# Two gated linear attentions on one core: the last stage rewritten as one list of steps in a joint order of all engines

## The chip, the cores and the metric

The kernel runs on one core of one Trainium2 chip. A core has a matrix engine (PE, whose weight loads the profile counts apart as PEld), a vector engine (DVE), a scalar engine (ACT), GpSimd (POOL) and a sync engine (SP). Here SP only issues transfers; ACT issues some besides its own work. Each engine works through its own instructions in the order in which they were written, and waits on semaphores for what the others must have done. The metric is the time of one execution in microseconds of device time; a time is the median over several executions.

## The reference, cut to what matters

Two branches A and B with weights of their own see the same input `x` of 2048 tokens by 448. Both are linear attentions with 16 heads of 28, and a gate mixes them:

```
qkv = x @ wqkv                        # per head: q, k, v of 28
pq, pk = q @ w_phi, k @ w_phi         # per head
phi = concat(softmax(p), softmax(-p)) # 56 features for q, and for k
kv, z = phi_k^T v, sum of phi_k
o = (phi_q kv) / (phi_q z + 1e-6)
a = o @ wo                            # branch A; b is branch B in the same way
out = g * a + (1 - g) * b,   g = sigmoid(sum(x * gate_w))
```

All is float32. Where the kernel multiplies by weights, it splits an operand into a high and a low part and adds three products.

## The kernel before, in words

The 2048 tokens are 16 tiles of 128, and the work goes by pairs of tiles, units 0 to 7 (`NU` = 8). The program has three stages.

The first makes branch A's keys and values. The second makes branch A's queries and its attention result unit by unit, and stores it to device memory (`od`), while branch B's keys and values are accumulated in PSUM. Both hold three PSUM pairs (tiles of two banks, `two`) that are used in turn, and two banks for the state `kv`.

The last stage makes branch B's queries and attention, joins A's and B's results (the gate is already in the weights of each), and multiplies by `wo`. Its steps for a unit `u` and its two tiles `t` = 2u and 2u+1:

- `proj`: 22 matmuls make a unit's projected queries in a PSUM pair. `q_front` takes the maximum of every head (DVE) and the differences to it (DVE, two instructions, into `uq`), and stores them by four transfers, two from SP and two from ACT. `q_load` reads them back in another layout (`tq`, SP).
- `q_exp0`, `q_min`, `q_exp1`, `q_turn`: ACT takes exponents, DVE the minimum, POOL the negated differences, ACT their exponents, and DVE turns the result by 32x32 blocks into `wtb`.
- `num`: the product of the features with the turned state `kvt` (PE, 32 matmuls over four banks). `b_turn` turns it back (DVE) into `ctr` or into a part of `wva`, which takes the place of a second `ctr`. `n_rec`, `n_den` and `weights` make the divisor and the gate's weights (DVE and POOL in turns).
- `b_mix`: for each tile POOL multiplies by the weights (`n_mul`, 896 columns) and adds the two halves into `osb` (`n_add`), beside which A's result has been loaded (`o_load`, SP).
- `o_turn`: DVE turns a tile's joined result, four of seven 128-column parts into a PSUM bank (`turned`, tile `pair`) and three into SBUF or into the first bank of `num`; ACT copies each as the high part. `low_first` (DVE) and `low_rest` (POOL for even tiles, DVE for odd ones) make the low part.
- `out_mm`: 21 matmuls, 7 high by high weights, 7 high by low weights, 7 low by high weights (`woh`, `wol`). `out_copy`: ACT copies the product to `obs`, SP stores it.

The order of the engines' work is the order in which Python calls these functions. At the start of the last stage the pools of the first two are closed and a new pool `stage3` takes their place: two pairs, whose first bank holds a product and whose second a turned tile, and four banks `num`. Then a loop takes the units one by one, and within it stands the whole of one unit's chain:

```
        if u <= NU:
            low_first(2 * u - 2)
        if u < NU:
            b_num(u)
        out_mm(2 * u - 3)
        if u < NU:
            b_turn(u)
```

Of the kernel before, what the change touches and what calls it, by code (L numbers as in the profile page):

```python
# [8 lines left out]
F32 = mybir.dt.float32  # L9
# [5 lines left out]
P = 128  # L15
# [9 lines left out]
WARM = 16  # L25
MID = 4


@with_exitstack
def hedgehog_mix(ctx: ExitStack, tc: tile.TileContext, xd, wv, wkt, wqt, wphi, wo, cmask, cpmask, out):  # L30
# [6 lines left out]
    one_stack, two_stack = ExitStack(), ExitStack()  # L37
    one = one_stack.enter_context(tc.tile_pool(name="one", bufs=1, space=bass.MemoryType.PSUM))
    two = two_stack.enter_context(tc.tile_pool(name="two", bufs=3, space=bass.MemoryType.PSUM))
# [78 lines left out]
    def two_tile():  # L118
        return two.tile([P, 2, 512], F32, name="two")
# [49 lines left out]
    def k_sums(k):  # L169
# [5 lines left out]
        nc.vector.reciprocal(rs, sm)  # L175
        phis[k] = es.pop(k)
        for s in range(2):
            e3 = e[:, s].rearrange("p (h f) -> p h f", f=DH)
            nc.gpsimd.tensor_tensor(e3, e3, rs[:, s, :, None].to_broadcast([P, HA, DH]), OP.mult)  # L179

# [7 lines left out]
    kvb = [one.tile([P, 512], F32, name=f"kv{b}") for b in range(2)]  # L188
    for b in range(2):
        nc.vector.memset(kvb[b], 0.0)  # L190
    kvp = [t[:, :H * DH // 2].rearrange("p (g s f) -> p g s f", g=4, f=DH) for t in kvb]
# [16 lines left out]
    def state_turn(b):  # L208
        nc.vector.transpose(kvt[b].rearrange("p s g m -> p (s g m)"), kvs[b].rearrange("p s g f -> p (s g f)"))

        nc.gpsimd.memset(kvt[b][:, :, :, DH + 1], 1.0)
        nc.gpsimd.tensor_scalar(kvt[b][:, 0, :, DH], kvt[b][:, 0, :, DH], 1e-6, None, op0=OP.add)

# [4 lines left out]
    def q_front(k, ps):  # L218
# [8 lines left out]
        for c in range(4):  # L227
            eng = nc.sync if c < 2 else nc.scalar
            eng.dma_start(qd[k][:, :, c].rearrange("r t x -> t r x"), u[32 * c:32 * c + 32].rearrange("p r g w f -> p r (g w f)"))

# [11 lines left out]
    def q_min(k):  # L242
        mn = work.tile([P, 4, 8], F32, name="qmn")
        nc.vector.tensor_reduce(mn, tq[k % 2].rearrange("p c g w f -> p c (g w) f"), AX.X, OP.min)  # L244
        nc.gpsimd.tensor_tensor(eq[:, 1, :, :, :DH], mn.rearrange("p c a -> p a c")[:, :, :, None].to_broadcast([P, 8, 4, DH]),  # L245
                                tview(k), OP.subtract)

# [26 lines left out]
    def n_rec(k):  # L274
        rs, dd, den = sms[k] = sums()
        cv = cview(k)
        nc.vector.reciprocal(rs, cv[:, :, :, :, DH + 1])  # L277
        nc.gpsimd.tensor_tensor(dd, cv[:, :, :, :, DH], rs, OP.mult)  # L278
        nc.gpsimd.tensor_tensor(den, dd[:, :, 0], dd[:, :, 1], OP.add)

# [220 lines left out]
    k, n, m = 2 * NU - 1, NU - 1, NU + 1  # L501
# [4 lines left out]
    def o_load(u):  # L506
        nc.sync.dma_start(osb[:, u % 2, :, 0:4, :], od[u].rearrange("p (a r f) -> p a r f", r=4, f=DH))

    pq = proj(2, wq[1], two_tile())
    k_sums(k)  # L510
    a_turn(n)
    n_rec(n)
    q_front(NU + 2, pq)
    q_load(NU + 2)
    q_exp0(m)
    q_min(m)
    q_exp1(m)
    n_den(n)
    pq = proj(3, wq[1], two_tile())
    kv_acc(k)  # L520
    state_copy(1)
    q_front(NU + 3, pq)
    q_load(NU + 3)
    state_turn(1)
    weights(n, nc.gpsimd)
    n_mul(n)
    a_add(n)
    q_turn(m)
    for u in range(2):
        o_load(u)  # L530
# [8 lines left out]
    hls = {}  # L539

    def turned(t, ps, lo, hi):

# [3 lines left out]
        nc.scalar.activation(hls[t][0][:, lo:hi], ps, AF.Copy)  # L546

    def low(t, ps, lo, hi, eng):
        eng.tensor_tensor(hls[t][1][:, lo:hi], ps, hls[t][0].bitcast(F32)[:, lo:hi], OP.subtract)  # L549


    def turn_of(t):
        return pairs[t % 2][:, 1].rearrange("p (k t) -> p k t", t=P)

    def rest_of(t):
        return nps[:, 0, :(7 - MID) * P].rearrange("p (k t) -> p k t", t=P) if t % 2 and t > 1 else oTs[t % 2]

    def o_turn(t):
        if t % 3 == 2:
            hls[t] = [ph.tile([P, 7, P], F32R, name=f"vs{i}", bufs=1) for i in range(2)]  # L560
        else:
            e = ph.tile([P, 2, 7, P], F32R, name="e")
            hls[t] = [e[:, i] for i in range(2)]
        turned(t, turn_of(t), 0, MID)
        turned(t, rest_of(t), MID, 7)

    def low_first(t):
        low(t, turn_of(t), 0, MID, nc.vector)

    def low_rest(t, eng):  # L570
        low(t, rest_of(t), MID, 7, eng)

    def out_mm(t):
        hi, lo = hls.pop(t)
        terms = [(x[:, c], w[:, c]) for x, w in ((hi, woh), (hi, wol), (lo, woh)) for c in range(7)]
        for n, (a, w) in enumerate(terms):
# [144 lines left out]
```

## Time and profile before

| | |
|---|---|
| time, median of 3 runs | 373.44 us (372.65 to 373.65) |
| profiled execution | 371.96 us, of which the span is 369.9 us |
| PE busy in the span | 349.8 us (95%) |
| DVE, POOL, ACT busy | 274.8 us (74%), 258.7 us (70%), 120.5 us (33%) |
| TensorE clock granted | 1.00 in the whole span |
| last stage, on PE | 245.12 us (its first projection) to 366.5 us (its last product) |

The profile is of one execution. A row of the timeline says when a group of like instructions starts, how long it lasts, the engine, the line in the kernel, what is written and read, and in brackets how long the engine stood idle before it and what released it. The chain of waits goes back from the last instruction, at each step to what released it. A line number belongs to the function printed above that holds it.

### The profile page before, as it was taken

The page shows a single profiled execution, that of the slowest core. Times are in us where ns is not written, and L with a number is a line of the kernel's source. Part 1 is how long each engine was busy: PE and PEld are TensorE (multiplying, and loading weights), DVE is VectorE, ACT ScalarE, POOL GpSimd, SP SyncE. Part 2 cuts the span into 40 slices and gives each one's busy share as a digit, 9 for nine tenths or more (in the row PEclk, how much of TensorE's full clock was granted, in tenths as well). Part 3 has the DMA queues.
Part 4 walks back from the last instruction along what each step waited for, and adds up shares of the span by engine and source line. Part 5 has one row for each costly group of instructions (what it writes and reads, how often), then busy time and mean ns, then how long its engine had stood idle before and what let it go on. Part 6 is the DMA issues. An engine that isn't in the chain of part 4 may idle for free. (4 is left out here: it accounts for less than half of the span.)

```text
span 369.9 us, 8408 instructions
## 1 busy us (share of the span) xinstructions
PE 349.8 (95%) x3584; PEld 305.6 (83%) x3584; DVE 274.8 (74%) x309; ACT 120.5 (33%) x169; POOL 258.7 (70%) x224
## 2 busy tenths in 40 slices
PE   6999999999989999899999999997996999999986
PEld 6898989889878888889898898987885887777875
DVE  3464853566298389898988989889789989997740
ACT  2545337221434142321314133122123434433231
POOL 2179496783657308997888988785686889886670
PEclk9999999999999999999999999999999999999999
DMA  8955227105353403133231313395575244231221
GB/s 222 315 192 166 109 84 205 50 1 166 135 175 116 137 4 105 51 101 101 101 91 62 100 64 92 98 351 187 182 214 164 76 151 152 76 92 54 80 76 50
DMA packets 33733, 45.75 MB, mean 124 GB/s; under 512 B 11408, under 2 KB 27008, under 8 KB 33408
## 3 DMA queue, kind: packets, MB, share of 16 engines
q1 hardware_dynamic: 28032, 41.02, 35.2%
q10 hardware_dynamic: 5664, 4.20, 3.5%
q8 instruction: 28, 0.46, 0.5%
q14 instruction: 9, 0.07, 0.1%
HBM read 27.29 MB, written 19.53 MB: 127 GB/s over the span
## 5 line engine op out<-in xcount | busy, mean ns | idle before, releaser
L179 POOL TENSOR_TENSOR e<-e,rs 128x896 f32<-128x896 f32 x32 | 53.9, 1704 | 23.1 <-DVE rs L175 23.1
L146 PE MATMUL two<-wka,xg 128*128 128x448 f32 x264 | 55.8, 366 | 0.7 <-ACT wka L128 0.5
L146 PEld LDWEIGHTS two<-wka,xg 128*128 128x128 f32 x264 | 48.8, 188 | 4.8 <-ACT wka L128 1.2
L183 ACT ACTIVATE vs<-two 128x896 f32<-128x896 f32 x16 | 14.8, 922 | 99.6 <-PE two L146 99.6
L174 DVE TENSOR_REDUCE sm<-e 128x32 f32<-128x896 f32 x32 | 33.1, 1078 | 12.8 <-ACT e L167 12.8
L577 PE MATMUL pair<-wkb,e 128*128 128x448 f32 x154 | 36.8, 376 | 5.4 <-DVE e L549 3.0
L146 PE MATMUL two<-wqa,xg 128*128 128x448 f32 x176 | 38.0, 371 | 0.3 <-DVE wka L129 0.3
L577 PEld LDWEIGHTS pair<-wkb,e 128*128 128x128 f32 x154 | 27.8, 188 | 12.2 <-DVE e L549 4.3
L146 PE MATMUL two<-wva,xg 128*128 128x450 f32 x176 | 37.4, 367 | 0.0
L146 PE MATMUL two<-wvb,xg 128*128 128x448 f32 x176 | 37.2, 366 | 0.0
L252 DVE STREAM_TRANSPOSE wtb<-xrb 128x2048 f32<-128x2048 f32 x16 | 36.8, 2300 | 0.5 <-ACT xrb L249 0.5
L146 PE MATMUL two<-wkb,xg 128*128 128x448 f32 x176 | 36.6, 362 | 0.0
L146 PEld LDWEIGHTS two<-wqa,xg 128*128 128x128 f32 x176 | 32.4, 188 | 3.9 <-DVE wka L129 0.8
L146 PEld LDWEIGHTS two<-wva,xg 128*128 128x128 f32 x176 | 33.2, 189 | 2.9
L146 PEld LDWEIGHTS two<-wvb,xg 128*128 128x128 f32 x176 | 33.0, 188 | 2.8
L146 PEld LDWEIGHTS two<-wkb,xg 128*128 128x128 f32 x176 | 33.0, 188 | 2.3
L245 POOL TENSOR_TENSOR xrb<-qmn,tq 128x896 f32<-128x896 f32 x16 | 28.1, 1757 | 6.6 <-DVE qmn L244 3.9
L167 ACT ACTIVATE e<-e 128x896 f32<-128x896 f32 x32 | 28.7, 944 | 11.8 <-POOL e L163 11.5
L163 POOL TENSOR_TENSOR e<-mx,e 128x896 f32<-128x896 f32 x16 | 27.2, 1703 | 5.2 <-DVE mx L162 5.0
L249 ACT ACTIVATE xrb<-xrb 128x896 f32<-128x896 f32 x16 | 15.3, 953 | 43.7 <-POOL xrb L245 43.7
L295 POOL TENSOR_TENSOR wva<-wva,cdd 128x896 f32<-128x896 f32 (+1 forms) x12 | 26.5, 2210 | 0.9
L295 POOL TENSOR_TENSOR ctr<-ctr,cdd 128x896 f32<-128x896 f32 (+1 forms) x12 | 26.6, 2213 | 0.6
(104 smaller groups left out, 602.4 us busy)
## 6 DMA issues: line engine op xcount, KB each, us to landing
tq<-qd SPq DMA_DIRECT2D x16, 448.0 KB, 3.5
qd<-uq SPq DMA_DIRECT2D x32, 112.0 KB, 2.5
qd<-uq ACTq DMA_DIRECT2D x32, 112.0 KB, 3.2
od<-wva SPq DMA_DIRECT2D x8, 448.0 KB, 2.5
wqa<-od SPq DMA_DIRECT2D x8, 448.0 KB, 5.6
out<-bd SPq DMA_DIRECT2D x16, 224.0 KB, 2.0
wod<-wtb SPq DMA_DIRECT2D x14, 224.0 KB, 2.0
xrb<-in_xt SPq DMA_DIRECT2D x2, 1024.0 KB, 7.0
```

The lines of the kernel that those rows point to most:

```text
L146: nc.tensor.matmul(ps[:, i, :n], x[:, xc, o:o + P], w[:, k, wc], start=j == 0, stop=j == len(terms) - 1)
L163: nc.gpsimd.tensor_tensor(e5[:, 1], mx[:, 1, :, :, None].to_broadcast([P, 2, H, DH]), e5[:, 0], OP.subtract)
L167: nc.scalar.activation(es[k][:, s], es[k][:, s], AF.Exp)
L174: nc.vector.tensor_reduce(sm[:, s], e[:, s].rearrange("p (h f) -> p h f", f=DH), AX.X, OP.add)
L179: nc.gpsimd.tensor_tensor(e3, e3, rs[:, s, :, None].to_broadcast([P, HA, DH]), OP.mult)
L183: nc.scalar.activation(v[:, :, :, :, :DH].rearrange("p w j q f -> p w (j q) f"), hb(ps[:, :, :D]), AF.Copy)
L245: nc.gpsimd.tensor_tensor(eq[:, 1, :, :, :DH], mn.rearrange("p c a -> p a c")[:, :, :, None].to_broadcast([P, 8, 4, DH]), tview(k), OP.sub ...
L249: nc.scalar.activation(eq[:, 1, :, :, :DH], eq[:, 1, :, :, :DH], AF.Exp)
L252: nc.vector.transpose(wtb[k % 2], eq.rearrange("p s a c f -> p (s a c f)"))
L295: nc.gpsimd.tensor_tensor(c3, c3, dd.to_broadcast([P, 8, hi - lo, DH]), OP.mult)
L577: nc.tensor.matmul(pairs[t % 2][:, 0, :D], a, w, start=n == 0, stop=n == len(terms) - 1)
```

## The change

The first two stages keep their instructions and the order of them. PSUM is laid out anew: the two state banks are one pair `kv` in a pool `base`, which also holds one of the three pairs; the other two pairs have pools of their own (`stacks`). The last stage is written as small functions (`acts`), and a string `STEPS` lists the calls of all engines in one order; two to three letters name a step, the number behind the point a unit or a tile. The names that the prediction uses: `q` projection, `qf` the old maximum and differences, `mx`, `cp`, `qs` the new ones, `sq`, `aq` the stores from SP and from ACT, `sl` the load back, `mn`, `ms`, `e1`, `qt` minimum, POOL's difference, exponent and turn, `sc` the copy of the state, `bt`, `nr`, `sm`, `nd`, `wt` turn and weights, `mu`, `ad` POOL's multiply and add, `so` the load of A's result, `oa`, `ob` the two turns of a joined tile, `ha`, `hb` their copies by ACT, `lf`, `lr` the two low parts, `oh` the 14 matmuls with the high part, `ol` the 7 with the low part, `oc`, `sw` copy and store of the product.

```
+FIRST = 1
+STEPS = """
+at q.2 ks q.3 na km qf.2 mn.1 aq.2 sq.2 e0.1 ms.1 kv qf.3 q.4 sc sa e1.1 st sq.3 aq.3 da qt.1 wa so.0 sl.2 ss ma num.0 qf.4
...
+"""
-    one = one_stack.enter_context(tc.tile_pool(name="one", bufs=1, space=bass.MemoryType.PSUM))
-    two = two_stack.enter_context(tc.tile_pool(name="two", bufs=3, space=bass.MemoryType.PSUM))
+    stacks = [ExitStack(), ExitStack()]
+    base = ctx.enter_context(tc.tile_pool(name="base", bufs=1, space=bass.MemoryType.PSUM))
+    twos = [base, *(s.enter_context(tc.tile_pool(name=f"two{i}", bufs=1, space=bass.MemoryType.PSUM, side=("left", "right")[i]))
+                    for i, s in enumerate(stacks))]
...
-    two_stack.close()
-    one_stack.close()
-    stage3 = ctx.enter_context(tc.tile_pool(name="stage3", bufs=1, space=bass.MemoryType.PSUM))
-    pair0 = stage3.tile([P, 2, 512], F32, name="pair0")
-    nps = stage3.tile([P, 4, 512], F32, name="num")
-    pairs = [stage3.tile([P, 2, 512], F32, name="pair1"), pair0]
...
+    A, B, C = (turn[0] + 2) % 3, turn[0], (turn[0] + 1) % 3
+    QBANK = {2: C, 3: A, 4: B, 5: A, 6: B, 7: A}
+    def single_banks(i):
+        stacks[i].close()
+        pool = ctx.enter_context(tc.tile_pool(name=f"single{i}", bufs=1, space=bass.MemoryType.PSUM, side=("left", "right")[i]))
+        j = 1 - i
+        turns[j], outs[j] = [pool.tile([P, 512], F32, name=f"{n}{j}") for n in ("turn", "out")]
+    def q(f):
+        qps[f] = proj(f, wq[1], two_tile(QBANK[f]))
+    def both(f):
+        reads[f] = reads.get(f, 0) + 1
+        if reads[f] == 2 and f > 5:
+            single_banks(7 - f)
+    def mx(f):
+        m = maxs[f] = work.tile([P, 2, H], F32, name="qmx")
+        nc.vector.tensor_reduce(m, hb(qps[f][:, :, :D]), AX.X, OP.max)
+        both(f)
+    def cp(f):
+        nc.scalar.activation(ub(f), hb(qps[f][:, :, :D]), AF.Copy)
+        both(f)
+    def qs(f):
+        nc.gpsimd.tensor_tensor(ub(f), ub(f), maxs[f][:, :, :, None].to_broadcast([P, 2, H, DH]), OP.subtract)
+    def sc():
+        state_copy(1)
+        nps.extend([two_tile(C), base.tile([P, 2, 512], F32, name="kv")])
+    def bt(u):
+        for i in range(2):
+            nc.vector.transpose(ctr[u % 2][:, 1024 * i:1024 * i + 1024], nps[i].rearrange("p r t -> p (r t)"))
+    def products(t, pairs):
+        hi, lo = hl(t)
+        for n, (x, w) in enumerate(pairs):
+            for c in range(7):
+                nc.tensor.matmul(outs[t % 2][:, :D], (hi, lo)[x][:, c], w[:, c], start=x == 0 and n == 0 and c == 0,
+                                 stop=x == 1 and c == 6)
+    def oh(t):
+        products(t, ((0, woh), (0, wol)))
+    def ol(t):
+        products(t, ((1, woh),))
+    def lr(t):
+        eng = nc.vector if t % 2 and t > 1 else nc.gpsimd
+        eng.tensor_tensor(hl(t)[1][:, MID:], rest_of(t), hl(t)[0].bitcast(F32)[:, MID:], OP.subtract)
+    for step in STEPS.split():
+        name, _, arg = step.partition(".")
+        acts[name](*([int(arg)] if arg else []))
```

`mx`, `cp` and `qs` are used for the last two projections, 6 and 7, alone: ACT copies the projection to `uq`, and POOL subtracts the maximum there. The other four keep `qf`. Numbered names below (`two_2734`, `e`, `vs_3001`) are buffers.

First place, DVE around the last two projections and the first turned tiles (`qmx` is a maximum, `uq` the differences, `ctr` a turned `num`, `pair` or `turn` a turned tile). Before:

```order
L222 TENSOR_REDUCE qmx<-pair_2738 128x32
L224 TENSOR_TENSOR uq_124<-pair_2738,qmx 128x16x28 x2
L545 STREAM_TRANSPOSE pair_2738<-wqa 128x512
L545 STREAM_TRANSPOSE wva<-wqa 128x384
L587 STREAM_TRANSPOSE ctr<-num 128x2048
L277 RECIPROCAL crs<-ctr 128x64
L244 TENSOR_REDUCE qmn<-tq_127 128x32
L549 TENSOR_TENSOR e<-pair_2738,e 128x512
```

Now:

```order
L682 STREAM_TRANSPOSE ctr<-two_2734 128x1024
L682 STREAM_TRANSPOSE ctr<-kv 128x1024
L330 RECIPROCAL crs<-ctr 128x64
L597 TENSOR_REDUCE qmx<-two_2868 128x32
L343 RECIPROCAL cden<-cden 128x32
L717 STREAM_TRANSPOSE turn_2943<-wqa 128x512
L717 STREAM_TRANSPOSE wva<-wqa 128x384
L597 TENSOR_REDUCE qmx<-two_2904 128x32
L717 STREAM_TRANSPOSE turn_2994<-wqa 128x512
L741 TENSOR_TENSOR e<-turn_2943,e 128x512
```

The second turned `num` stands ahead of both last maxima and of the first turned tile, and the differences `uq` are gone from DVE.

Second place, DVE in one unit of the steady part, from the turned `num` on. Before:

```order
L587 STREAM_TRANSPOSE ctr<-num 128x2048
L277 RECIPROCAL crs<-ctr 128x64
L545 STREAM_TRANSPOSE pair_2736<-wqa 128x512
L545 STREAM_TRANSPOSE num<-wqa 128x384
L282 RECIPROCAL cden<-cden 128x32
L549 TENSOR_TENSOR vs_3191<-pair_2736,vs_3190 128x512
L549 TENSOR_TENSOR vs_3191<-num,vs_3190 128x384
L252 STREAM_TRANSPOSE wtb_119<-xrb 128x2048
L545 STREAM_TRANSPOSE pair_2738<-wqa 128x512
L545 STREAM_TRANSPOSE wva<-wqa 128x384
L244 TENSOR_REDUCE qmn<-tq_126 128x32
L549 TENSOR_TENSOR e<-pair_2738,e 128x512
```

Now, from the end of the unit ahead of it:

```order
L306 STREAM_TRANSPOSE wtb_121<-xrb 128x2048
L717 STREAM_TRANSPOSE turn_2943<-wqa 128x512
L717 STREAM_TRANSPOSE wva<-wqa 128x384
L682 STREAM_TRANSPOSE ctr<-two_2734 128x1024
L682 STREAM_TRANSPOSE ctr<-kv 128x1024
L330 RECIPROCAL crs<-ctr 128x64
L717 STREAM_TRANSPOSE turn_2994<-wqa 128x512
L717 STREAM_TRANSPOSE kv<-wqa 128x384
L343 RECIPROCAL cden<-cden 128x32
L741 TENSOR_TENSOR e<-turn_2943,e 128x512
```

The even tile's low part (`e<-pair_2738`, now `e<-turn_2943`) stood ahead of the next turned `num`; now it stands behind it, and the turned `num` follows the turned tile at once.

Third place, POOL from one minimum's difference to the next (`xrb<-qmn,tq`). Before:

```order
L245 TENSOR_TENSOR xrb<-qmn,tq_127 128x32x28
L278 TENSOR_TENSOR cdd<-ctr,crs 128x64
L279 TENSOR_TENSOR cden<-cdd 128x32
L549 TENSOR_TENSOR e<-wva,e 128x384
L289 TENSOR_TENSOR cden<-cden,gate 128x32
L290 TENSOR_TENSOR cdd<-crs,cden 128x64
L295 TENSOR_TENSOR ctr<-ctr,cdd 128x8x4x28
L299 TENSOR_TENSOR wqa<-ctr 128x4x4x28
L295 TENSOR_TENSOR ctr<-ctr,cdd 128x8x4x28
L299 TENSOR_TENSOR wqa<-ctr 128x4x4x28
L245 TENSOR_TENSOR xrb<-qmn,tq_126 128x32x28
```

Now, where the second of the two moved differences stands:

```order
L296 TENSOR_TENSOR xrb<-qmn,tq_130 128x32x28
L335 TENSOR_TENSOR cdd<-ctr,crs 128x64
L336 TENSOR_TENSOR cden<-cdd 128x32
L745 TENSOR_TENSOR e<-wva,e 128x384
L350 TENSOR_TENSOR cden<-cden,gate 128x32
L351 TENSOR_TENSOR cdd<-crs,cden 128x64
L356 TENSOR_TENSOR ctr<-ctr,cdd 128x8x4x28
L360 TENSOR_TENSOR wqa<-ctr 128x4x4x28
L356 TENSOR_TENSOR ctr<-ctr,cdd 128x8x4x28
L360 TENSOR_TENSOR wqa<-ctr 128x4x4x28
L296 TENSOR_TENSOR xrb<-qmn,tq_129 128x32x28
L605 TENSOR_TENSOR uq_128<-uq_128,qmx 128x2x16x28
```

POOL keeps the order within a unit; the new row is added behind it. On PE the six projections keep their order, in the pairs of the earlier stages, and behind the last of them a third `num` stands ahead of the first product.

More of the change, by code (lines that the diff above doesn't have):

```diff
@@ new lines, in hedgehog_mix @@
+    assert (A, B) == (1, 2)
+    nps, turns, outs = [], [None, None], [None, None]
+    QBANK = {2: C, 3: A, 4: B, 5: A, 6: B, 7: A}
[6 more added lines that the diff above has]
+        qps[f] = proj(f, wq[1], two_tile(QBANK[f]))
@@ L558, in o_turn, with oa_, ob_ @@
[L558 to L563, printed above, removed]
+    def oa_(t):
         turned(t, turn_of(t), 0, MID)
+    def ob_(t):
         turned(t, rest_of(t), MID, 7)
[L567 to L571, printed above, removed]
```

287 lines of the change are left out of this document (144 added, 143 removed).

## The prediction

> **What bounds the kernel now.** I read the busy shares of the page first: PE is busy for 95% of the span, at a clock of 1.00 throughout. So only PE's idle time and lost steps can be won, and only in the stage that changes. The busy times of that stretch, from the stage's first projection on PE to its last product (columns: stretch, length, then busy us of PE, PEld, DVE, ACT, POOL with instruction counts, clock, DMA share, GB/s):
>
> ```profile
> 245.12:366.57 121.45, 112.02 (x1052) 93.29 (x1044) 97.50 (x119) 37.27 (x65) 87.07 (x91) 1.00 0.42 129
> ```
>
> PE idles for 9.43 of 121.45 us. Next, what PE waits for there (us in total, times, longest):
>
> ```profile
> PE pair L577 <- DVE e L549: 3.0, 1, 3.0
> PE pair L577 <- POOL e L549: 2.5, 4, 0.6
> PE pair L146 <- ACT kvs L206: 1.9, 1, 1.9
> PE pair L577 <- DVE vs L549: 1.3, 1, 1.3
> PE pair L577 <- POOL vs L549: 0.8, 2, 0.6
> ```
>
> These make up the 9.4 us: two waits at the front (1.9 and 3.0), one of some 0.6 in each of five units, and 1.3 near the end. PE's timeline prices the work between them:
>
> ```profile
> 245.12 9.08 PE L146 MATMUL two<-wka,xg 128*128 128x448 f32 x44
> 254.13 0.99 PE L201 MATMUL kv<-e,vs 128*29 128x56 f32 x64
> 257.05 4.68 PE L146 MATMUL pair<-wka,xg 128*128 128x448 f32 x22 [1.92 <-ACT kvs L206]
> ...
> 281.16 1.70 PE L577 MATMUL pair<-wkb,e 128*128 128x448 f32 x7 [2.95 <-DVE e L549]
> ...
> 305.02 0.99 PE L577 MATMUL pair<-wkb,e 128*128 128x448 f32 x4
> 306.64 0.88 PE L577 MATMUL pair<-wkb,e 128*128 128x448 f32 x3 [0.63 <-POOL e L549]
> 307.44 1.50 PE L264 MATMUL num<-wtb,kvt 32*32 32x256 f32 x64
> ...
> 318.57 1.49 PE L264 MATMUL num<-wtb,kvt 32*32 32x256 f32 x64
> 320.00 1.69 PE L577 MATMUL pair<-wkb,e 128*128 128x448 f32 x7
> ...
> 324.37 1.67 PE L577 MATMUL pair<-wkb,vs 128*128 128x448 f32 x7
> ...
> 364.92 1.61 PE L577 MATMUL pair<-wkb,e 128*128 128x448 f32 x7
> ```
>
> From start to start a projection costs 4.50 us (9.01 for two), `num` 1.43 (318.57 to 320.00), a product of 21 matmuls without a wait 4.37 (320.00 to 324.37), `kv` 0.92 (its 0.99 less the overlap that the other rows show). A wait costs more than its idle time: the seven matmuls from 305.02 take 2.42 us where a free seven take 1.41 to 1.46, so 0.63 of idling cost about 1.0; measured from the moment the matmul was due, about 0.8 of lateness and 0.2 to get going again.
>
> Last, the chain of waits, over one unit of the steady part (start, us, what):
>
> ```profile
> 302.04 2.23 DVE ctr L587
> ...
> 304.29 0.56 DVE crs L277
> 304.86 0.07 issue
> 304.93 0.37 POOL cdd L278
> ...
> 307.29 1.71 POOL ctr L295
> ...
> 309.06 1.16 POOL wqa L299
> ...
> 310.24 0.74 DVE pair L545
> ...
> 311.01 0.47 ACT e L546
> ...
> 311.91 0.55 ACT bd L580
> ...
> 312.48 0.69 DVE e L549
> 313.18 2.23 DVE wva L587
> ```
>
> The turned `num` of one unit leads over POOL's multiply and add, the turned tile, ACT's copies and the low part straight to the next turned `num`: a loop of 11.14 us, because DVE's order puts the low part ahead of it. PE needs only 1.43 + 2 × 4.37 = 10.17 for a unit. It waits because the loop is longer. The same unit by engines:
>
> ```profile
> 302.04:313.18 11.14, 10.51 (x107) 8.46 (x106) 10.26 (x13) 4.76 (x9) 9.56 (x11) 1.00 0.41 125
> ```
>
> DVE's 10.26 and POOL's 9.56 (about 10 with the gap of 0.07 that stands ahead of most of its instructions) lie hardly below 11.14, and right at PE's 10.17: once the loop is cut, three engines bind almost equally.
>
> **The floor.** Without any wait PE needs 6 × 4.50 + 0.92 + 8 × 1.43 + 16 × 4.37 = 109.3 us from 245.12, and would end at 354.4. Its last group now ends at 366.5 (364.92 + 1.61). So at most 12.1 us are to be had; the change removes no PE work.
>
> **The change, part by part.**
>
> The banks. The 1.92 ended with ACT's copy of the state, which the closed pools made the projection wait for. Now projection 4 writes a pair that the stage's first DVE step has read 8 us before, and the copy moves ahead of the second exponent on ACT. The wait goes. Next late is `num.0`, by way of POOL's last touch of `kvt`: about 258.4, against PE's 259.6. Cost nothing, covered by projection 4 itself.
>
> The third `num` ahead of the first product. It moves 1.43 us of PE work to where PE idled 2.95. The first product now waits for ACT's copy of projection 7, which ends on PE near 276.1, and for two copies of the turned tile behind it on ACT:
>
> ```profile
> L183 ACT ACTIVATE vs<-two 128x896 f32<-128x896 f32 x16 | 14.8, 922 | 99.6 <-PE two L146 99.6
> ...
> L179 POOL TENSOR_TENSOR e<-e,rs 128x896 f32<-128x896 f32 x32 | 53.9, 1704 | 23.1 <-DVE rs L175 23.1
> ...
> L224 DVE TENSOR_TENSOR uq<-pair,qmx x8: 615/620/625, 262.9 to 282.9; 128x448 f32<-128x448 f32 x8
> L546 ACT ACTIVATE e<-pair 128x512 fp32r<-128x512 f32 x11 | 6.6, 598 | 28.8 <-DVE pair L545 28.8
> ```
>
> 276.1 + 0.95 + 0.6 = 277.7, while `num.2` ends at 277.5: late by 0.15. Before, the product began at 281.16 without that `num`, so the front returns 4.9 us.
>
> The moved differences. DVE loses four instructions of 0.62 (2.5 us), ACT gains two copies of 0.92 (the `vs` copy is the same shape out of PSUM; ACT is 31% busy here), POOL two of 1.70 to 1.76 (nearest: 1704 ns above). The copy has no trace of before: down to 0.60 (the 128x512 copy), up to twice the 0.92 for its strided writes; I take 0.92, the same shape; the bounds move the first product by -0.3 to +0.9. On ACT the stores `aq.6` and `aq.7` wait for POOL's differences, and `oc`, `hb`, `e1` queue behind them: no cost while `qs` is on time (`qs.6` ends near 287.0, PE wants `hb.3` at 290.9).
>
> The Trainium skill, Perfetto Trace Analysis, Optimizing Scalar/DVE Operations, says that GpSimd and DVE share an SBUF read port, so that moving work between the two "might not help". In this stretch POOL's differences took 1747 to 1760 ns each and DVE's 615 to 625, while both were busy for most of the time; no row shows one stretched by the other, so the trace does not bear the rule out here. By the rule the sum would have DVE held for 3.5 us instead of 2.5 freed.
>
> The loop. Now the turned `num` follows the turned tile at once: 302.04 to 310.24 is 8.2, and the two turns of the tile add 1.1: a loop of 9.3, under PE's 10.17. Five units had lost about 1.0 each: 5 us, of which the engines' loads may take back some. Splitting the turned `num` in two costs nothing measurable (the earlier stage's pair of 1024 columns takes 2.31, the single one 2.30).
>
> What is late next, found by following the list by hand with these durations:
> - `ol.4`. From the first difference of the stage that POOL can start without a gap (`ms.2`, about 265.7, behind DVE's `qf.4`, `bt.0` and minimum) to the end of `lr.4` POOL has 4 differences and one `qs` of 1.75, 6 multiplies of 1.77 and 6 adds of 1.2 with their gaps, 3 `sm` of 0.65, 3 `wt` of 0.75 and 4 `lr` of 0.97: 34.7 us, until 300.4. `nd.3` and `lf.4` on DVE wait for the `sm.3` among them and end at the same time. PE wants `ol.4` at 245.12 + 27.0 + 0.92 + 4 × 1.43 + 4 × 4.37 + 2.93 = 299.2, plus 0.5 of earlier waits: late by 0.7. This is the price of `qs.6`, and of the difference `ms.5` that stands ahead of `sm.3`.
> - `num.3` waits for `lr.3` behind `nd.2` on DVE: 0.25; `ol.7` for `lf.7` behind a turned `num`: 0.25; `ol.2` for `lr.2`: 0.1.
> Together with the first product 1.45, and 0.2 each to get going again: 2.45.
>
> The tail. The last two stores change places on SP:
>
> ```profile
> L581 SPq DMA_DIRECT2D out<-bd x16: 332/332/375, 290.1 to 367.1; - x16
> DMA to landing us min/median/max: 1.9/2.0/2.1
> ```
>
> `sw.14` is now issued behind `sw.15`, which waits for the last copy, and the program ends one issue later: 0.35.
>
> The loads at the front. `sl.2` is moved behind `sq.3` and `so.0` on SP:
>
> ```profile
> 256.32 0.34 SPq L232 DMA_DIRECT2D tq<-qd  x1
> 256.75 0.86 SPq L229 DMA_DIRECT2D qd<-uq  x2
> ...
> tq<-qd SPq DMA_DIRECT2D x5, 448.0 KB, 3.9
> wqa<-od SPq DMA_DIRECT2D x4, 448.0 KB, 6.4
> ```
>
> It leaves about 257.7 instead of 256.3. If it lands 3.9 later, at 261.6, the minimum at 264.7 does not see it; if it has to stand behind the 6.4 of `so.0` first, it lands at 267.6 to 268, and everything that POOL does from `ms.2` on starts up to 2.8 later. I take nothing, since the two share the queues rather than wait for each other's end, and keep 2.8 for the range. The other stores and loads have 3 us and more in hand by the same reckoning (`sl.7` lands near 318, `mn.7` stands at 322).
>
> **Sum.** 12.1 - 2.45 - 0.35 = 9.3 us less. Against the profiled execution of 371.96: 362.7. That execution stands 1.5 under the median of the runs, so for the median 373.44 - 9.3 = 364.1.
>
> **Rivals.**
> - *The waits come back unit by unit.* DVE at 10.26 and POOL at 10 have nothing in hand against 10.17, and every hop between them adds some hundredths. If each of five units keeps its 1.0, 5 us go: 373.44 - 4.9 - 1.3 + 0.35 = 367.6. For it: the load row. Against it: most of DVE's waits in that unit hang on the loop that is cut. 0.2.
> - *The load of `tq` comes late behind `so.0`.* 2.8 less of gain: 366.9. For it: the 6.4. Against it: the list has spare time on DVE there (projection 7 wants `qf.5` only at 271.6). 0.15.
> - *POOL's difference holds DVE.* If the two engines exclude each other in the moved differences, DVE is 3.5 late at `bt.2` and `oa.6`, most of it passed on: up to 367.6. The even durations above speak against it. By the Trainium skill's sentence on the shared port, Perfetto Trace Analysis, Optimizing Scalar/DVE Operations, this is how it would go. 0.03.
> - *Slower: ACT's queue stands behind POOL.* `aq.6` waits on ACT for `qs.6`, and the product copies, `hb.3` and the exponents queue behind it. PE has 3.9 us in hand there (287.0 against 290.9), and 9.3 of gain to lose: from `qs.6` later than about 300 on the kernel is slower; at 305, 378. Only a POOL that is 13 us late at that point does this, and its row of work up to there is 20 us long. 0.05.
> - *The gaps only move.* The list cuts the named waits, and others of the same size arise: 373.4. With three engines at 10 of 10.17 not excluded. 0.04.
> The forecast, between 361.6 and 366, has 0.5; 0.03 are left for mixtures.
>
> **How the numbers follow.** A difference of 0.3% (1.1 us) is about what a measurement of this kernel can tell from none. The low end is the floor without any wait, 373.44 - 12.1 + 0.35 = 361.7, and a tenth below for rounding: 361.6. The high end takes in the returning waits, the late load and the held DVE with half a us over: 368.2. Faster 0.90 (all but the last two rivals and a share of the mixtures), same 0.04, slower 0.06.
>
> **What would show it.** In the profile after, PE's idle time in the stage falls from 9.4 to 1 to 3 us; no projection waits for ACT's state copy; the first product starts at 277.5 to 278.5; starts of `num` in the steady part lie 10.2 to 10.5 apart instead of 11.1; the last product ends at 356 to 358; the largest remaining PE wait is near 300, for DVE or POOL low parts. Wrong would be: a PE wait for a DMA-fed step (`wtb`, `tq`), POOL rows longer than 1.76, or `num` still 11 apart.

## The result, and the profile after

The changed kernel takes 360.11 us (median of 4 runs, 359.97 to 360.84) beside 373.46 us of the kernel before on the same chip: a ratio of 0.9651, 95% interval 0.9631 to 0.967. Three single executions in the runs below took 429, 563 and 858 us, the first two at a granted clock of 0.76 and 0.56; like the few that lay over 1.5% above the fastest of their kernel, they are in no comparison. The forecast of 364.1 had the right sign and most of the size, but the time lies 1.5 us below the low end of the range.

The profiled execution took 360.23 us, its span 358.0 us. The row of busy times of the last stage, from its first projection to its last product (columns as in the prediction):

```profile
244.10:354.00 109.90, 109.59 (x1052) 94.29 (x1044) 93.35 (x123) 39.03 (x66) 90.16 (x93) 1.00 0.46 141
```

PE idles for 0.3 of 109.90 us, where it idled for 9.43 of 121.45. Its waits in that stretch are this one row:

```profile
PE out L751 <- DVE vs L741: 0.2, 1, 0.2
```

The places that the prediction named, in PE's timeline:

```profile
244.10 9.08 PE L172 MATMUL two<-wka,xg 128*128 128x448 f32 x44
253.11 0.99 PE L236 MATMUL kv<-e,vs 128*29 128x56 f32 x64
254.03 4.68 PE L172 MATMUL two<-wka,xg 128*128 128x448 f32 x22
...
276.67 1.69 PE L751 MATMUL out<-wkb,e 128*128 128x448 f32 x7
...
288.51 1.69 PE L751 MATMUL out<-wkb,vs 128*128 128x448 f32 x7 [0.20 <-DVE vs L741]
...
298.84 1.71 PE L751 MATMUL out<-wkb,e 128*128 128x448 f32 x7
...
352.36 1.61 PE L751 MATMUL out<-wkb,e 128*128 128x448 f32 x7
```

The projection at 254.03 follows `kv` at once: the 1.92 for the copy of the state is gone. The first product starts 32.57 us after the stage where it started 36.04 after it, although a third `num` now stands ahead of it. The only bracket is 0.20, ahead of `ol.2`. The last matmul ends at 353.97; the stage has 109.87 us, where it had 121.41, and the floor worked out in the prediction is 109.3.

The two profiled executions differ by 11.73 us: 1.02 because the stage starts earlier (244.10 against 245.12; the first two stages keep their work, see the runs with a longer warm-up below), 11.54 in the stage, 0.66 given back between the last matmul and the end of the span (4.03 against 3.37), 0.17 given back outside the span. The medians differ by 13.35, since the profiled execution of before stood 1.5 under its median and that of after stands 0.1 over its own. Before's 373.46 is also the highest of its medians: on the four chips of the runs below it has 371.4 to 371.6.

### The profile page after: what moved, and what is told of

The parts are those of the page before. It is cut to its first block, busy times and chain, and to the rows that moved or that the text cites. A ratio compares the mean times of both kernels' runs of the same rounds, so it can differ in the third digit from the quotient of the medians.

```text
span 358.0 us, 8412 instructions
## 1 busy us (share of the span) xinstructions
PE 345.9 (97%) x3584; PEld 305.2 (85%) x3584; DVE 271.5 (76%) x312; ACT 122.2 (34%) x171; POOL 261.8 (73%) x226
## 4 chain that ended last, share of the span: by engine, by line
PE 62%; POOL 13%; DVE 10%; DMA 6%; issue 4%; ACT 3%; SPq 1%; POOLq 0%; DVEq 0%; ACTq 0%
PE two L172 34%; PE out L751 16%; POOL e L211 6%; PE two L318 4%; PE two L149 3%; PE kv L236 3%; DVE sm L202 2%; POOL xg L112 2%; DMA qd<-uq 2%; POOL e L189 2%; POOL xg L110 1%; DMA tq<-qd 1%; DVE wtb L306 1%; DMA gate<-gd 1%; DMA mask<-in_cmask 1%
## 5 line engine op out<-in xcount | busy, mean ns | idle before, releaser
L172 PE MATMUL two<-wka,xg 128*128 128x448 f32 x352 | 74.2, 366 | 0.6 <-ACT wka L154 0.4
L172 PEld LDWEIGHTS two<-wka,xg 128*128 128x128 f32 x352 | 65.1, 188 | 6.7 <-ACT wka L154 1.1
L751 PE MATMUL out<-wkb,e 128*128 128x448 f32 x154 | 34.7, 369 | 0.1
L751 PEld LDWEIGHTS out<-wkb,e 128*128 128x128 f32 x154 | 28.5, 188 | 4.0 <-issue 0.8
L263 DVE TENSOR_REDUCE qmx<-two 128x32 f32<-128x896 f32 x14 | 15.1, 1082 | 16.9 <-PE two L172 16.9
```

Source lines behind the costliest of these rows:

```text
L172: nc.tensor.matmul(ps[:, i, :n], x[:, xc, o:o + P], w[:, k, wc], start=j == 0, stop=j == len(terms) - 1)
L263: nc.vector.tensor_reduce(mx, p4, AX.X, OP.max)
L751: nc.tensor.matmul(outs[t % 2][:, :D], (hi, lo)[x][:, c], w[:, c], start=x == 0 and n == 0 and c == 0, stop=x == 1 and c == 6)
```

## The experiments

All ratios are to the kernel before, run beside the kernel on the same chip. "Stage" is from the start of the stage's first projection to the end of the last matmul, in the profiled execution.

| kernel | median us | ratio, 95% interval | stage us |
|---|---|---|---|
| before | 371.4 to 371.6 on these chips | 1 | 121.41 |
| changed, again (r5) | 361.09 | 0.9718, 0.9689 to 0.9748 | 109.90 |
| third `num` late (e1; r6 the same) | 361.45; 361.3 | 0.9708, 0.9676 to 0.974; 0.9717, 0.9681 to 0.9752 | -; 110.75 |
| low part first (e2) | 360.25 | 0.9685, 0.9657 to 0.9712 | 110.59 |
| differences on DVE (e3) | 360.68 | 0.9696, 0.9664 to 0.9728 | 111.38 |
| all three undone (t9; u14 the same) | 362.99; 362.81 | 0.9767, 0.9731 to 0.9802; 0.9765, 0.9728 to 0.9803 | -; 112.20 |
| before, loop cut (e4) | 369.73 | 0.993, 0.99 to 0.9961 | 120.61, with two stretches at half clock |
| before, product copy later (t10) | 368.63 | 0.9943, 0.9911 to 0.9974 | 119.60, with one such stretch |
| before, front cut (u13) | 372.0 | 1.0009, 0.9983 to 1.0035 | 121.67 |
| before, longer warm-up (t11) | 369.77 | 0.9957, 0.9933 to 0.998 | 121.12 |
| changed, longer warm-up (r7) | 357.94 | 0.9644, 0.9611 to 0.9677 | 109.86 |
| changed, stores in order (r8) | 359.62 | 0.9681, 0.9648 to 0.9714 | 109.85 |
| changed, both (t12) | 357.75 | 0.9637, 0.9608 to 0.9666 | 109.91 |

The stage is the sharper measure: in the five profiles that leave it as the change made it, it has 109.85 to 109.91 us. The medians carry the start of the program as well. The stages of e4 and t10 can't be compared so closely: PE's clock was halved for 3.41 us twice in the one and once in the other, and not at all in the stage of the other profiles.

**Third `num` behind the first product.** One step of the list moves:

```
-... nr.1 mx.6 sm.1 ad.1 nd.1 num.2 cp.7 ... sl.5 mn.4 ol.0 mu.3 ...
+... nr.1 mx.6 sm.1 ad.1 nd.1 cp.7 ... sl.5 mn.4 ol.0 num.2 mu.3 ...
```

> The changed kernel with the third num put back behind the first product; nothing else moved. Front theory (the third num fills time in which PE waits for the first turned tile): PE idles about 1.5 us ahead of the first product and does the 1.43 us of num later, so +1.4 us against the changed kernel, about 361.5. Rival (the front's slack is taken up later, because DVE or POOL bind there): no change, 360.1.

A second run of the same kernel, which gave the profile read here:

> The changed kernel with the third num put back behind the first product, once more, for an undisturbed profile. Front theory: the stage takes 1.4 us longer than the changed kernel's 109.9 us (111.3), with one PE wait of about 1.5 us ahead of the first product. Rival (slack taken up elsewhere): 109.9.

The waits of PE in the stage, of the second run:

```profile
PE out L751 <- ACT e L735: 1.5, 1, 1.5
```

PE idles for 1.5 where `num.2` had stood, for ACT's copy of the turned tile, and the stage is 0.9 longer, between the two forecasts. The medians can't tell this from no change. So the third `num` does fill the idle time, but the place is worth 0.9, not the 2.95 that PE idled there before.

**Low parts ahead of the turned `num` again.** The changed kernel's list, with the order on DVE that the prediction held to be the cause of the loop of 11.14 us:

```
-... ob.2 bt.2 ol.1 ... sm.2 lf.2 ...   (and lf.4, lf.6 in the same way)
+... ob.2 lf.2 bt.2 ol.1 ... sm.2 ...
```

> The changed kernel with the even tile's low part put back ahead of the turned num on DVE in units 2, 3 and 4 (lf.2, lf.4, lf.6 ahead of bt.2, bt.3, bt.4). Loop theory (this order closes the loop that made a unit 11.14 us): units 3 and 4 grow by about 1 us each, +1 to +2 us, about 361.5, with PE waits for low parts or wtb coming back near there. Rival (units have enough in hand, since other steps are also spread over units): under +0.4 us.

DVE's timeline, the first halves of three turned `num` and the low part ahead of one of them:

```profile
282.73 1.23 DVE L682 STREAM_TRANSPOSE wva<-two 128x1024 f32<-128x1024 f32 x1
...
292.49 0.69 DVE L741 TENSOR_TENSOR e<-turn,e 128x512 fp32r<-128x512 f32 x1 [0.22 <-ACT e L735]
293.10 1.24 DVE L682 STREAM_TRANSPOSE ctr<-two 128x1024 f32<-128x1024 f32 x1
...
303.58 1.24 DVE L682 STREAM_TRANSPOSE wva<-two 128x1024 f32<-128x1024 f32 x1
```

The turned `num` come 10.4 and 10.5 us apart, not 11.14 (in the changed kernel, at the same places, 10.0 and 10.1), and the stage is only 0.7 longer, between the two forecasts. The low part waits 0.22 for ACT's copy of the turned tile. In the kernel before ACT's copy of the previous product stood between the two: it is in the prediction's own chain, at 311.91, between the copy `e` at 311.01 and the low part at 312.48. So the low part's place alone doesn't make the loop of 11.14.

**ACT's product copy, in the kernel before.** This copy alone is moved:

```
     for u in range(2, NU + 2):
         if u <= NU:
             low_first(2 * u - 2)
+        if u > 2:
+            out_copy(2 * u - 4)
 ...
-        if u <= NU:
-            out_copy(2 * u - 2)
```

> The kernel before with ACT's copy of the product 2u-2 moved behind the next unit's copy of the turned tile, so that it no longer stands between that copy and the low part. Theory (with the result of the changed kernel whose low parts stood first, 10.4 us from turned num to turned num where the kernel before has 11.1): this copy is 0.5 to 0.7 us of the loop of 11.14, num comes every 10.4 to 10.6 us, and 2.5 to 4 us go: 367.5 to 369 against 371.5. Rival, DVE's order alone sets the loop, as the prediction has it: num stays 11.1 apart, no change. Rival, the product's bank comes free later and PE waits for ACT instead: 372 or more.

PE's timeline over the loop's units:

```profile
284.26 1.50 PE L264 MATMUL num<-wtb,kvt 32*32 32x256 f32 x64
...
294.43 1.49 PE L264 MATMUL num<-wtb,kvt 32*32 32x256 f32 x64
...
302.33 1.69 PE L577 MATMUL pair<-wkb,e 128*128 128x448 f32 x7 [1.93 <-ACT bd L580]
...
306.80 1.50 PE L264 MATMUL num<-wtb,kvt 32*32 32x256 f32 x64
...
329.00 1.50 PE L264 MATMUL num<-wtb,kvt 32*32 32x256 f32 x64
...
339.16 1.50 PE L264 MATMUL num<-wtb,kvt 32*32 32x256 f32 x64
```

ACT's, over the same place:

```profile
300.89 0.95 ACT L249 ACTIVATE xrb<-xrb 128x896 f32<-128x896 f32 x1 [2.06 <-POOL xrb L245]
301.75 0.53 ACT L580 ACTIVATE bd<-pair 128x448 f32<-128x448 f32 x1
```

Theory and last rival both hold. From 284.26 and from 329.00 `num` comes after 10.17 and 10.16 us, which is just PE's work; the same units took 10.60 and 11.13 before. There the loop is cut. But the copy now stands on ACT behind an exponent that waits 2.06 for POOL, and PE waits for it three times (1.93, 0.45, 0.96), because each product has the one bank. Of the loop's gain 2.8 us of the median is left, and 1.8 us of stage. The stage would have gained up to 3.3, an estimate: at half clock the first product took 6.00 us (278.26 to 284.26) where it took 4.47 before (281.16 to 285.63).

**The loop cut at DVE, in the kernel before.** The low part moves behind the turned `num`:

```
         if u <= NU:
-            low_first(2 * u - 2)
...
         if u <= NU:
+            low_first(2 * u - 2)
             low_rest(2 * u - 2, nc.gpsimd)
```

> The kernel before with one move alone: in the loop over units the even tile's low part stands behind the turned num instead of ahead of it. Loop theory: a unit falls from 11.14 to about 10.2 us in units 3 to 7, so -4 to -5 us, about 368.9, with the front's waits of 1.9 and 3.0 us unchanged. Rival (DVE at 10.26 and POOL at 9.56 us of work in a unit of 11.14 bind as soon as the loop is cut): -2 us or less.

PE's timeline, first the projection behind the state's copy, then a product of the loop:

```profile
255.55 6.28 PE L146 MATMUL pair<-wka,xg 128*128 128x448 f32 x22 [1.93 <-ACT kvs L206]
...
293.22 2.53 PE L577 MATMUL pair<-wkb,vs 128*128 128x448 f32 x7 [1.86 <-DVE vs L549]
295.55 2.33 PE L577 MATMUL pair<-wvb,vs 128*128 128x448 f32 x7
```

The five waits of 0.6 for POOL are gone, and waits of 1.86, 0.72 and 0.16 for DVE's low parts have come, which the prediction's account of the loop has no place for. In the two units without one, `num` comes after 10.17 and 10.16 us (299.22 to 309.40, 331.07 to 341.23), so this step, too, cuts the loop when it alone is moved. Two stretches run slowly: the projection takes 6.28 where it took 4.68 before, after the same wait, and fourteen matmuls take some 4.5 us where they take 3. The rows of busy times have the granted clock in the third column from the end:

```profile
256.23:259.64 3.41, 3.41 (x10) 3.00 (x10) 1.94 (x1) 0.00 (x0) 3.17 (x4) 0.50 0.78 252
293.78:297.19 3.41, 3.41 (x11) 3.02 (x10) 3.41 (x6) 1.52 (x3) 2.97 (x5) 0.50 0.17 62
```

The stage gains 0.8 net, the median 1.9, as little as the rival had it. The slow stretches cost the stage about 1.6 and 1.5 us, and before's profile has none there; without them it would have gained up to 3.9, an estimate. So it stays open how much of the missing gain is due to DVE's load, and how much to the clock. A wait of nearly 2 us on PE can thus cost a further 1.5 us by the clock. It need not: the profiled execution of before kept 1.00 after 1.92 and 2.95. The Trainium skill, TensorE: Matmul & The Clock Gate, Part 1, has the clock fall to half after an idle window of about 3.4 us; here a wait of 1.9 sufficed.

**The front cut, in the kernel before.** One DVE instruction moves, so that the first product need not wait for the low part behind the turned `num`:

```
     o_turn(0)
+    low_first(0)
     b_turn(1)
     b_make(3)
     low_rest(0, nc.gpsimd)
-    low_first(0)
```

> The kernel before with the first tile's low part on DVE ahead of the second unit's turned num instead of behind it, one DVE instruction in another place. Theory, the front and the loop are separate losses of about 3 and 5 us: the first product, which waited 2.95 us for this low part, follows projection 7 at once (near 278.2 where it was 281.16), num still comes every 11.1 us, the stage is 118 to 119 instead of 121.1 to 121.4, and 2 to 3 us go: 368.5 to 369.5 against 371.5. Rival, the loop's first turn starts from the turned num, which is now 1 us later, and the wait only moves to the next product: no change, or up to 1 slower.

PE's timeline:

```profile
278.25 1.61 PE L577 MATMUL pair<-wkb,e 128*128 128x448 f32 x7
...
281.10 0.97 PE L577 MATMUL pair<-wkb,e 128*128 128x448 f32 x4
284.39 0.88 PE L577 MATMUL pair<-wkb,e 128*128 128x448 f32 x3 [2.32 <-POOL e L549]
```

The first product starts at 278.25, as expected, without the wait of 2.95. Its last three matmuls then wait 2.32 for POOL's part of the low part, and nothing is won: the stage has 121.67, the ratio is 1.0009. The rival was right that the gap only moves, though it lands on POOL within the same product.

**The moved differences back on DVE.** In the list `qf.6` stands for `mx.6` and `cp.6`, `qf.7` for those of 7, and `qs.6`, `qs.7` go:

```
-... cp.6 bt.1 ... mx.6 sm.1 ... cp.7 ... mx.7 ... qs.6 ... qs.7
+... bt.1 ... qf.6 sm.1 ... qf.7 ...
```

> The changed kernel with the differences of projections 6 and 7 back on DVE (maximum and two differences each at the place of mx; no copy by ACT, no difference by POOL). If DVE binds behind the front, its 2.3 us more come back in the end: +1 to +2.3 us, about 361.5 to 362.4. If POOL binds, it gains 3.5 us and the time stays or falls by a few tenths. If PE binds alone with time in hand on both, the time stays at 360.1.

PE's waits in the stage:

```profile
PE out L753 <- DVE vs L743: 1.0, 1, 1.0
PE out L753 <- ACT e L737: 0.4, 1, 0.4
PE out L753 <- DVE e L743: 0.2, 1, 0.2
```

PE waits for DVE's low parts, and the stage is 1.5 longer. So the differences on GpSimd do free DVE, as the first of the three forecasts had it; the medians can't tell it.

**All three undone at once.**

> The changed kernel with three of its parts undone at once: the third num behind the first product, the low parts lf.2, lf.4 and lf.6 ahead of the turned num, and both moved differences back on DVE. Undone alone they lengthened the stage by 0.9 (110.75 against 109.87), 0.7 (110.59) and 1.5 us (111.38). Theory, the parts add: stage 112.9 to 113.2, about 364.2 us (3.1 over the changed kernel). Rival, each part was cheap alone because the others had left room, so that together they cost as much as the waits of the kernel before: stage 115 to 121, 367 or more. Rival, they hide in the same wait: stage 111.4, about 362.5.

A second run of the same kernel, which gave the profile read here:

> The same kernel as the one with three parts undone, whose profiled execution had a granted clock of 0.56. Theory, the parts add (0.9, 0.7 and 1.5): stage 112.9 to 113.2. Rival, two of them hide in the same wait: stage 111.4 to 112. Rival, shared room: 115 or more, which the earlier median of 363.0 already speaks against.

PE's waits in the stage:

```profile
PE out L750 <- ACT e L734: 1.9, 1, 1.9
PE out L750 <- DVE e L740: 0.2, 1, 0.2
```

The stage has 112.20: 2.3 more than the changed kernel, where the three alone sum to 3.1. The waits ahead of the first product add up (1.5 and 0.4 alone, 1.9 here), but the 1.0 for DVE's low part that the differences cost alone is gone: in part the three hide in the same wait, and they stay far from 121. The other 9.2 us lie in what the three leave as it is: the pair for projection 4 (1.9, by the row at 254.03), and the rest of the joint order and of the separate banks, which was not taken apart further.

**The changed kernel again.**

> The changed kernel as it is, for a comparison on the same chip as the three below, and for a second profile. If the 1.0 us by which the last stage began earlier in its first profile (244.10 against 245.12) is luck of the first two stages, the start moves again by up to some us while the stage itself stays at 109.9 us from its first projection to the end of its last matmul. If the new PSUM layout had made the first stages faster, the start stays near 244.1.

The stage has 109.90 with the same single wait of 0.2; the program takes 1 us longer than in its first profile, and its stage starts at 245.06, so the earlier start of 244.10 was luck and not the new banks. On this chip the change is worth 10.4 us.

**The start.** `WARM` sets the number of transposes that PE does ahead of its first matmuls:

```
-WARM = 16
+WARM = 28
```

> The changed kernel with 28 instead of 16 transposes ahead of its first real matmuls, so that PE does not idle from 5.0 to 7.0 us. If the first 32 small matmuls take 5.4 to 6.8 us (3.83 later in the program) because the clock is low after that idle time, they fall to about 4 us, and the time by 1.5 to 2 us, with less scatter. Rival (these transposes don't hold the clock up, or the data come late): no change, and the group still takes over 5 us.

> The kernel before with 28 instead of 16 transposes ahead of the first matmuls. Theory, the clock at the start costs both kernels the same: the 32 fold matmuls take 3.8 instead of about 6.8 us, the stage stays at 121.4, and about 3 us go: 368.4. Then the change is worth 10.5 (against 357.9 of the changed kernel with 28) where the start is the same for both. Rival, the kernel before loses in its other stages by waits of its own: then its stage starts later than 242.2 (245.12 less 3) and the distance to 357.9 stays above 12.

The program's first 32 matmuls (the fold) in PE's timelines, one row each from before, the changed kernel, the same again, the changed kernel with 28, and before with 28:

```profile
6.86 6.80 PE L123 MATMUL two<-bd,wtb 112*128 112x112 f32 x32 [1.84 <-DVE bd L313]
```
```profile
7.02 5.45 PE L149 MATMUL two<-bd,wtb 112*128 112x112 f32 x32 [2.00 <-DVE bd L374]
```
```profile
6.88 7.13 PE L149 MATMUL two<-bd,wtb 112*128 112x112 f32 x32 [1.87 <-DVE bd L374]
```
```profile
6.91 3.83 PE L149 MATMUL two<-bd,wtb 112*128 112x112 f32 x32 [0.90 <-DVE bd L374]
```
```profile
6.97 3.83 PE L123 MATMUL two<-bd,wtb 112*128 112x112 f32 x32 [0.65 <-DVE bd L313]
```

With 16 transposes the same kernel's group took 5.45 in one execution and 7.13 in another; with 28 it took 3.83 in both kernels. With 16 the changed kernel's first projection then starts at 12.89 or at 14.20, and its two profiled executions, whose stages are alike, took 360.23 and 361.25 us. The Trainium skill, TensorE: Matmul & The Clock Gate, Part 1, has the warm-up as about 3.4 us of time that differs from run to run. These rows agree that it differs; the 3.30 us lost in the second execution (7.13 less 3.83) is more than 3.4 us at half clock would lose, some 1.7.

Not all of this reaches the end in before, whose fold is 2.97 us shorter with 28. The waits of PE in the first two stages, of before and of before with 28:

```profile
PE kv L201 <- POOL e L179: 3.2, 5, 1.5
```
```profile
PE kv L201 <- POOL e L179: 4.3, 5, 1.9
```

Before's stage starts at 243.33, later than the 242.2 of the theory: its earlier PE waits longer for POOL, and it gains 1.7 us of the median. The changed kernel gained 3.1; such waits come to 3.4 and 3.0 in its two profiles with 16 transposes, and to 1.7 and 2.9 in its two with 28. Why the two kernels differ is not shown. With the start alike, before and changed kernel lie 12.0 us apart on one chip (369.77, and 357.75 with the order of the last stores changed too), of which the stage has 11.2 (121.12 and 109.91).

**The last stores.**

```
-... lf.15 ol.14 oh.15 oc.14 ol.15 oc.15 sw.15 sw.14
+... lf.15 ol.14 oh.15 oc.14 ol.15 oc.15 sw.14 sw.15
```

> The changed kernel with its last two stores in the order sw.14, sw.15. If the exchange costs one issue at the end, as the prediction had it, -0.35 us, and the time from PE's end to the end of the span falls from 4.0 to about 3.4 us. Rival: 0.

> The changed kernel with 28 transposes at the start and the last two stores in the order of their copies. Theory, the two add: 361.1 less 3.1 and 0.6, 357.3 to 357.5, with a span near 354. Rival, the end of the program is not the issue of the store but its landing, which the order does not change: 357.9.

The end of the last copy and the issues behind it, of the changed kernel:

```profile
354.05 0.54 ACT L761 ACTIVATE bd<-out 128x448 f32<-128x448 f32 x1 [3.72 <-PE out L751]
354.62 0.81 SPq L765 DMA_DIRECT2D out<-bd  x2
```

The same of the changed kernel with both edits:

```profile
351.96 0.54 ACT L761 ACTIVATE bd<-out 128x448 f32<-128x448 f32 x1 [3.72 <-PE out L751]
352.53 0.33 SPq L765 DMA_DIRECT2D out<-bd  x1
```

Two stores are issued behind the last copy in the one, a single one in the other. From the last matmul to the end of the span it is 4.03 and 4.04 in the changed kernel's two profiles, 3.43 and 3.42 with the stores in order: 0.6. The median with the stores in order, 359.62, is 1.5 under the changed kernel's on the same chip, more than the tail explains. By the medians the kernel with both edits, 357.75, and the one with the longer warm-up alone, 357.94, are the same.

## Why the prediction was right, and where it was wrong

- *The floor was right.* PE bounds the stage, and the floor of 109.3 stands 0.6 under the 109.87 measured.
- *The first step that failed: the late steps, 2.45 us.* PE's waits for them came to 0.2, and all that lies over the floor is 0.6. Of the 1.45 of named waits the first product's 0.15 came (`num.2` to the first product took 1.56 instead of 1.42) and `ol.2`'s 0.1 came as 0.20; `num.3`, `ol.4` and `ol.7` waited for nothing, and so the restarts of 0.2 each fell away with them. The largest, `ol.4`'s 0.7, hung on POOL's list. POOL's timeline from `ms.2` to `lr.4`, and what follows it:

```profile
264.98 1.76 POOL L296 TENSOR_TENSOR xrb<-qmn,tq 128x896 f32<-128x896 f32 x1 [0.31 <-issue]
...
276.22 1.70 POOL L356 TENSOR_TENSOR ctr<-ctr,cdd 128x896 f32<-128x896 f32 x1
277.88 1.02 POOL L745 TENSOR_TENSOR e<-wva,e 128x384 fp32r<-128x384 f32 x1
278.86 1.17 POOL L360 TENSOR_TENSOR wqa<-ctr 128x448 f32<-128x448 f32 x1
279.98 1.71 POOL L356 TENSOR_TENSOR ctr<-ctr,cdd 128x896 f32<-128x896 f32 x1
...
283.72 1.72 POOL L605 TENSOR_TENSOR uq<-uq,qmx 128x896 f32<-128x896 f32 x1
...
297.81 1.01 POOL L745 TENSOR_TENSOR e<-wva,e 128x384 fp32r<-128x384 f32 x1
...
299.53 1.71 POOL L356 TENSOR_TENSOR ctr<-ctr,cdd 128x896 f32<-128x896 f32 x1
301.31 1.14 POOL L360 TENSOR_TENSOR wqa<-ctr 128x448 f32<-128x448 f32 x1
```

  From 264.98 to 298.82 it is 33.84 us, where 34.7 was reckoned. POOL began 0.3 later than reckoned in the stage and still ended as `ol.4` was due, at 298.82 against 298.84. Taken from start to start, the six adds came to 0.4 less than reckoned (1.11 to 1.12 each but for one of 1.23, against 1.2), the six multiplies to 0.3 less, the four differences and `qs` to 0.2 less, the four low parts to 0.1 more. The reckoning took every multiply at 1.77. A multiply with its own add behind it takes that, 1.78 (299.53 to 301.31); with another step behind it, it takes 1.66 (276.22 to 277.88). That the add waits for the multiply's result is the likely reason, but not shown: the two multiplies from 267.45 to 270.89 take 3.44, one of them 1.78, though the add behind them reads the first one's result alone. The Trainium skill, Perfetto Trace Analysis, GPSIMD Engine Instruction, also wants GpSimd timed by start-to-start spacing; here the durations alone, 1.70 and 1.71, hide the difference.
- *The tail* was taken at 0.35 and is 0.66 in the profiles; the kernel with the stores in order has 3.43 where before has 3.37, which shows that the order is nearly the whole of it.
- *The sum for stage and tail* was 9.3 and is 10.9 (11.54 less 0.66). This 1.6 comes from the two points above: 1.9 too much for the late steps, 0.3 too little for the tail.
- *The step that put the time below the range: from profile to median.* The prediction added 1.5, and kept the stages ahead as they were. The late steps can't have done it, since the low end holds none: with stage and tail as measured, 373.44 less 11.54 plus 0.66 is 362.6, inside the range. The other 2.5 of the 4.0 us missed are the base: the changed kernel's executions didn't keep the 1.5, and its stage began 1.0 earlier. On the chip of the second profile, where before has 371.5, the 9.3 less would have been 362.2, and 361.09 was measured. Executions of before alone go from 367.5 to 373.7 on these chips, so the low end, worked out to a tenth from the floor, left out the spread that the start makes.
- *The loop.* Its end was foretold: `num` follows PE. Its starts lie 10.34, 8.68, 10.11 and 11.72 apart from 290.13 on, not 10.2 to 10.5, because the list puts unequal PE work between them. The cause was put on DVE's order alone. In the kernel before, moving either the low part or ACT's product copy lets `num` come after 10.16 or 10.17 us where no new wait arises, and putting the low parts back ahead in the changed kernel makes it 10.4 to 10.5 from turned `num` to turned `num`: low part and product copy were on the loop together.
- *The front.* The 1.92 went as told, and ACT's copies of the last projections took the 0.92 that was assumed. The 2.95 was counted as a gain of its own; in the kernel before it isn't one, since taking this low part alone out of the way gives 0.
- *Rivals.* No wait came back unit by unit. The load of `tq` cost nothing: ACT's exponent waited 7.4 us for it, until 262.79, but no PE, DVE or POOL wait for a DMA stands in the stage. The differences on GpSimd ran 1.70 to 1.72 each and no row of DVE beside them was stretched (turned halves 1.20 to 1.21 as elsewhere), so the sentence of the Trainium skill, Perfetto Trace Analysis, Optimizing Scalar/DVE Operations, on the shared port isn't borne out by these instructions. ACT's store behind `qs.6` went out at 285.47, 0.03 after the difference ended.

## What to carry to other kernels

When the bounding engine idles in many small gaps, the gaps are not separate sums: cutting one of them in the kernel before gave 0 (front), 2.8 (product copy) and 1.9 us (low part) of the median, and the joint order with its new banks gave 10.4. Work out the floor of the bounding engine first; if a hand trace of the new order finds waits of some tenths, price an engine's queue by start-to-start times, and each step by what stands behind it, since 0.9 us over 34 decided here whether PE waits. A range around a median must hold the spread that the start of the program makes, which is larger than such terms.

## What the runs showed of the hardware

- After PE waits of 1.9 to 2.6 us the granted clock fell to 0.50 for 3.41 us in some executions (256.23 and 293.78 in the kernel with the loop cut, 278.25 in the one with the product copy later), and stayed at 1.00 after 1.92 and 2.95 in another. In part these profiles tell why: the changes of the clock within the program lie whole multiples of 3.41 us apart (from 256.23 to 293.78 it is 37.55, eleven times that), and what tells the cases apart is PE's busy time in the 3.41 us ahead of a possible change. With 1.48, 1.55 and 0.79 us the clock fell; with 1.59 and 1.60, where a wait of 2.63 or 1.95 lay across two such stretches, it did not. At the program's start it fell behind 1.62 us as well (5.23 to 8.64 in the changed kernel's first profile), so busy time isn't all that counts. Rows of the loop cut (a wait, and no fall behind it) and of the product copy (a wait, and the fall behind it):

```profile
276.71:280.12 3.41, 1.59 (x8) 1.14 (x7) 3.38 (x3) 1.44 (x3) 0.59 (x2) 1.00 0.36 107
```
```profile
274.84:278.25 3.41, 0.79 (x4) 0.38 (x3) 3.38 (x5) 0.63 (x1) 1.11 (x3) 1.00 0.18 57
278.25:281.66 3.41, 3.40 (x9) 3.06 (x10) 3.34 (x6) 1.03 (x2) 3.25 (x5) 0.50 0.33 78
```

  No run set out to test this.
- At the very start the granted clock in the records need not show the slow stretch: in the changed kernel's second profile the 32 matmuls of the fold took 7.10 us at a recorded clock of 1.00. In its first profile, where they took 5.45, the record does show 0.50 for 3.41 us of them:

```profile
6.90:14.00 7.10, 7.10 (x32) 6.88 (x32) 0.00 (x0) 0.77 (x1) 0.00 (x0) 1.00 1.06 352
```
```profile
8.64:12.05 3.41, 3.41 (x18) 3.41 (x18) 0.00 (x0) 0.13 (x1) 0.00 (x0) 0.50 1.07 370
```

- Twelve more transposes on a PE that stood idle anyway take 1.6 to 3.3 us off the fold: 5.45 to 7.13 with 16, 3.83 in all three profiles with 28. They also shorten PE's idle time ahead of the fold from 1.8 to 2.0 us to 0.5 to 0.9; no run tells whether the added work or the shorter idle time does it.
